# Sharing batch 0's v casts among three engines, two tiles for batch 1's transposes, and a later place for batch 2's kv matmuls

## The chip, the cores and the metric

One core of one Trainium2 chip. The metric is the device time of one execution, in microseconds (us), median of several executions. Engines: PE (TensorE; PEld is its weight load), DVE (VectorE), ACT (ScalarE), POOL (GpSimd), SP (SyncE, which issues most transfers). The profiles below are of different executions, on several chips.

## The reference

Linear attention for 8 batches, 8 heads, 576 tokens, head size 64, then a feed-forward pair with exact Gelu:

```python
q_s = softmax(q, over head_dim);  k_s = softmax(k, over tokens)
kv  = einsum('bhsd,bhse->bhde', k_s, v)          # 64x64 for each head
x   = einsum('bhsd,bhde->bhse', q_s, kv)         # -> 4608 tokens x 512
out = gelu(x @ w_in) @ w_out                      # 512 -> 2048 -> 512, float32 in and out
```

## The kernel before

Everything is cast to bf16 on the chip. PE runs, for each batch of 512 tokens, 64 matmuls of the first layer (`h_phase`), 64 of the second (`y_phase`), and between them the small ones: 72 for kv, 8 for x, and for batches 0 and 1 also 16 transposes of q (the later batches get theirs by DMA). In the code, `ek` is exp(k), `qT` the transposed q, `xT` the transposed x, which the first layer reads. For batches 0 and 1 all of this must wait for first loads: q, k, v of batch 0, then the weights. The parts that the change touches, with cuts marked:

```python
def cast_v(b, hp, eng=nc.vector):              # v, f32 -> bf16, one pair of heads
    eng.tensor_copy(out=v_aug[b % 2][:, hp, :, 0:D],
                    in_=st[b]["vf"][:, hp, :].rearrange("p (n d) -> p n d", n=NS))

def tp_mm(b, half):                            # 8 transposes of q into PSUM
    ...
    if b == 1:
        if half == 0:
            st[b]["tp"] = psum_a.tile([128, 2, J, 2, 128], BF16, tag="a2", name="tp")
        ps = st[b]["tp"][:, half]              # both halves in one tile
    ...
# ---- the front
tp_mm(0, 0); tp_evac(0, 0, "s")
table(AF.Gelu)                                 # loads Gelu's table on ScalarE
warm(2)
cast_v(0, 0)
for hp in range(1, HP):
    cast_v(0, hp, nc.gpsimd)
cast_wi(0, wi[0], "p"); cast_wi(1, wi[1], "p") # weight chunks 0, 1 on GpSimd
tp_mm(0, 1); warm(2)
...                                            # kv, x of batch 0, then the first layer
h_phase(0, {0: [cast_wi(2, "v")], 2: [cast_wi(3, "v")], ...})   # chunks 2 to 4 on VectorE
...
# ---- batch 1 in batch 0's second layer
tp_step(1, 0); tp_step(1, 1)                   # 8 transposes, copy out, twice
cast_v(1, 3)
y_part(12, range(J)); y_part(13, range(J))
kv_step(1)
...
y_phase(1, {(1, 12): [kv_step(2)], ...})       # batch 2's kv behind 29 matmuls
```

The softmax here doesn't subtract the row's maximum and nothing guards it: scores larger than these inputs give would overflow.

## Time and profile before

| | before |
|---|---|
| time, median of 6 runs | 281.69 us (281.43 to 282.00) |
| span of the profiled run | 280.1 us |
| PE busy | 271.0 us, 97% |
| first layer of batch 0 starts | 14.75 us |
| second layer of batch 0 starts | 29.29 us |
| batch 1's second eight transposes start | 41.05 us |
| batch 2's kv matmuls start | 66.92 us |

PE sets the time. What counts is when it starts each of its blocks, so the timeline of PE (start, duration, line, operation, count) is the view to read, and the other engines only where one of them releases PE. The lines at the three places are in the prediction below; three more:

```profile
29.29 10.52 PE L310 MATMUL ps<-wo_bf,g 128*128 128x512 bf16 x48
...
67.64 5.57 PE L310 MATMUL ps<-wo_bf,g 128*128 128x512 bf16 x25
73.14 0.63 PE L256 MATMUL ps<-qT,kvc 64*64 64x512 bf16 x8
```

A wide matmul (512 columns) occupies PE for 0.216 us from start to start; its listed 379 ns are its whole latency, pipelined.

### The profile page before, as it was taken

What the parts mean: (1) busy time and instruction counts of PE and PEld (TensorE: products, weight loads), DVE (VectorE), ACT (ScalarE), POOL (GpSimd) and SP (SyncE); (2) the same over time, 40 slices, a digit from 0 to 9 for tenths busy, and PEclk for the clock granted to TensorE, in tenths of its full rate; (3) what the DMA queues carried; (4) which work ended last, traced back from release to release, by engine and by line L of the source; (5) the groups of instructions that cost most, each with busy time, mean ns of one, the idle gap of its engine ahead of it and who ended that gap; (6) DMA issues with size and microseconds to landing.
All of it is one profiled execution on the core that took longest, in us unless ns stands there. A gap on an engine that the chain in (4) does not pass through costs nothing.

```text
span 280.1 us, 4564 instructions
## 1 busy us (share of the span) xinstructions
PE 271.0 (97%) x1922; PEld 125.2 (45%) x1922; DVE 102.2 (37%) x152; ACT 157.0 (56%) x243; POOL 33.0 (12%) x25
## 2 busy tenths in 40 slices
PE   7699989999999999999999999999999999999995
PEld 3344444444544444444444444444444444444443
DVE  3767477308763530074007500552005200230012
ACT  5747664779466915692469436852683264036400
POOL 1530050002020040005000500050005000000000
PEclk9999999999999999999999999999999999999999
DMA  6999999961997129911991189126501500120033
GB/s 235 380 404 427 400 401 407 399 250 43 268 390 91 41 76 240 357 41 42 259 372 41 42 209 375 53 77 171 131 0 75 150 2 0 75 77 0 0 77 76
DMA packets 44996, 50.10 MB, mean 179 GB/s; under 512 B 20400, under 2 KB 29872, under 8 KB 44720
## 3 DMA queue, kind: packets, MB, share of 16 engines
q1 hardware_dynamic: 44688, 49.68, 53.4%
q8 instruction: 15, 0.25, 0.4%
q10 hardware_dynamic: 288, 0.13, 0.2%
q14 instruction: 5, 0.04, 0.1%
HBM read 36.70 MB, written 9.44 MB: 165 GB/s over the span
## 4 chain that ended last, share of the span: by engine, by line
PE 75%; DMA 18%; SPq 2%; ACT 2%; ACTq 0%; issue 0%; DVE 0%
PE ps L310 36%; PE ps L300 35%; DMA w<-in_moe_w_in_dram 6%; DMA f<-in_v_dram 4%; DMA w<-in_moe_w_out_dram 3%; DMA out_dram<-y_sb 3%; SPq L98 2%; DMA touch<-in_moe_w_out_dram 2%; PE kv L166 1%; PE ps L332 1%; PE ps L256 1%; ACT ek L138 1%; ACT e L133 1%; ACTq L435 0%; ACT L133 0%
## 5 line engine op out<-in xcount | busy, mean ns | idle before, releaser
L300 PE MATMUL ps<-xT,wi_bf 128*128 128x512 bf16 x576 | 126.4, 379 | 0.2
L310 PE MATMUL ps<-wo_bf,g 128*128 128x512 bf16 x560 | 124.2, 379 | 0.0
L305 ACT ACTIVATE g<-ps 128x512 bf16<-128x512 f32 x144 | 85.2, 597 | 69.3 <-PE ps L300 69.3
L300 PEld LDWEIGHTS <-wi_bf 128*128 128x128 bf16 x576 | 56.1, 98 | 69.0 <-DVE wi_bf L383 1.0
L310 PEld LDWEIGHTS <-g 128*128 128x128 bf16 x560 | 54.0, 98 | 64.6 <-issue 0.8
L317 DVE COPY y_sb<-ps 128x512 f32<-128x512 f32 x35 | 23.8, 686 | 80.9 <-PE ps L310 80.7
L198 POOL TENSOR_TENSOR e<-e,recq 128x2048 bf16<-128x2048 bf16 (+1 forms) x9 | 25.7, 2857 | 179.2 <-DVE recq L197 151.0
L145 DVE CAST v_aug<-f 128x576 bf16<-128x576 f32 x26 | 17.9, 745 | 46.4 <-DMA f<-in_v_dram 46.4
L196 DVE TENSOR_REDUCE qsum<-e 128x16 f32<-128x1024 bf16 (+1 forms) x13 | 21.0, 1614 | 15.0 <-ACT e L133 15.0
L282 ACT CAST xT<-ps 128x512 bf16<-128x512 f32 x19 | 10.2, 589 | 27.9 <-PE ps L256 18.2
L133 ACT ACTIVATE e<-f 128x512 bf16<-128x512 f32 (+1 forms) x42 | 20.5, 556 | 2.4 <-DMA f<-in_q_dram 2.1
L138 ACT ACTIVATE ek<-f 128x2304 bf16<-128x2304 f32 (+1 forms) x10 | 17.2, 1730 | 1.9 <-DMA f<-in_k_dram 1.9
L280 DVE CAST xT<-ps 128x512 bf16<-128x512 f32 x15 | 9.7, 686 | 17.7 <-PE ps L256 14.8
L79 ACT ACT_TABLE_LOAD x9 | 11.5, 1283 | 2.8 <-issue 2.6
L133 ACT ACT_TABLE_LOAD x7 | 9.0, 1283 | 0.1
L417 PE MATMUL ps<-zeros 128*128 128x512 f32 (+1 forms) x14 | 7.1, 647 | 1.5 <-DVE zeros L449 1.5
L383 DVE CAST wi_bf<-w 128x512 bf16<-128x512 f32 x12 | 7.4, 660 | 2.5 <-DMA w<-in_moe_w_in_dram 2.2
L166 PEld LDWEIGHTS <-ek 64*64 64x64 bf16 x576 | 6.3, 105 | 3.0 <-issue 1.4
L166 PE MATMUL kv<-v_aug,ek 64*64 64x65 bf16 x576 | 6.9, 193 | 0.3
L198 DVE TENSOR_TENSOR e<-e,recq 128x1024 bf16<-128x1024 bf16 x4 | 6.4, 1608 | 0.1
L256 PE MATMUL ps<-qT,kvc 64*64 64x512 bf16 x60 | 5.0, 390 | 1.0 <-DVE kvc L177 1.0
L410 DVE CAST wo_bf<-w 128x2048 bf16<-128x2048 f32 (+1 forms) x4 | 4.4, 1090 | 3.8 <-DMA w<-in_moe_w_out_dram 3.8
(35 smaller groups left out, 42.4 us busy)
## 6 DMA issues: line engine op xcount, KB each, us to landing
out_dram<-y_sb SPq DMA_DIRECT2D x32, 256.0 KB, 2.3
f<-in_k_dram SPq DMA_DIRECT2D x6, 1152.0 KB, 9.7
f<-in_v_dram SPq DMA_DIRECT2D x6, 1152.0 KB, 11.8
f<-in_q_dram SPq DMA_DIRECT2D x6, 1024.0 KB, 7.5
w<-in_moe_w_in_dram SPq DMA_DIRECT2D x6, 512.0 KB, 8.9
f<-in_k_dram SPq DMA_DIRECT2D x4, 576.0 KB, 10.1
f<-in_v_dram SPq DMA_DIRECT2D x8, 288.0 KB, 7.9
f<-in_q_dram SPq DMA_DIRECT2D x4, 512.0 KB, 12.5
```

The costliest lines, as they stand in the source:

```text
L79: nc.scalar.activation(out=scr[:, 1:2], in_=scr[:, 0:1], func=func)
L133: nc.scalar.activation(out=dst[:, i], in_=src[:, u], func=AF.Exp)
L138: nc.scalar.activation(out=ek[b % 2][:, i:i + n], in_=st[b]["kf"][:, i:i + n].rearrange("p x (n d) -> p x n d", n=NS), func=AF.Exp,)
L145: eng.tensor_copy(out=v_aug[b % 2][:, hp, :, 0:D], in_=st[b]["vf"][:, hp, :].rearrange("p (n d) -> p n d", n=NS),)
L166: nc.tensor.matmul(ps[c, i, half, 0:D + 1], ek[b % 2][pr, hp, n, :], v_aug[b % 2][pr, hp, n, 0:D + 1], start=(n == 0), stop=(n == NS - 1),)
L196: nc.vector.reduce_sum(out=qsum, in_=eq[:, :, hs, :], axis=AX.X)
L198: eng.tensor_tensor(out=eq[:, :, hs, :], in0=eq[:, :, hs, :], in1=recq.unsqueeze(3).to_broadcast([128, J, w, D]), op=ALU.mult,)
L282: nc.scalar.copy(out=st[b]["xT"][:, hp, :], in_=ps)
L300: nc.tensor.matmul(ps, wi_bf[:, dm, t * 128:(t + 1) * 128], xT[:, dm, :], start=(dm == 0), stop=(dm == NDM - 1),)
L305: nc.scalar.activation(out=g[:, t, :], in_=ps, func=AF.Gelu)
L310: nc.tensor.matmul(ps, st[c]["g"][:, t, j * 128:(j + 1) * 128], wo_bf[:, t, :], start=(t == 0), stop=(t == NDF - 1),)
L317: nc.vector.tensor_copy(out=y_sb, in_=ps)
```

## The change

Three separate edits. (1) The front: batch 0's v casts go to POOL, DVE and ACT, so that each is cast as it lands; the last pair is loaded and cast in two token groups (5 and 4 of 9); Gelu's table load moves behind ACT's cast. (2) Batch 1's two halves of transposes get tiles of their own. (3) Batch 2's kv matmuls move two matmuls later.

```diff
-            nc.sync.dma_start(out=f[:, i * n:(i + 1) * n, :], in_=src[:, i * n:(i + 1) * n, :])
+            if b == 0 and name == "v" and i == parts - 1:
+                for c in (slice(0, 5 * D), slice(5 * D, NS * D)):
+                    nc.sync.dma_start(out=f[:, i, c], in_=src[:, i, c])
+            else:
+                nc.sync.dma_start(out=f[:, i * n:(i + 1) * n, :], in_=src[:, i * n:(i + 1) * n, :])
...
-    def cast_v(b, hp, eng=nc.vector):
+    def cast_v(b, hp, eng=nc.vector, n0=0, n1=NS):        # body: tokens n0 to n1, ACT by copy
...
-        if b == 1:
-            if half == 0:
-                st[b]["tp"] = psum_a.tile([128, 2, J, 2, 128], BF16, tag="a2", name="tp")
-            ps = st[b]["tp"][:, half]
+        if b == 1 and half == 1:
+            ps = psum_a.tile([128, 2, J, 2, 128], BF16, tag="a2", name="tp")[:, 0]
         else:                                              # half 0: psum_a, tag "a"
...
+    warm(2)
+    cast_v(0, 0, nc.gpsimd)
+    cast_v(0, 1)
+    cast_v(0, 2, nc.scalar)
+    cast_v(0, 3, nc.gpsimd, 0, 5)
+    cast_v(0, 3, nc.gpsimd, 5, NS)
     table(AF.Gelu)
-    warm(2)
-    cast_v(0, 0)
-    for hp in range(1, HP):
-        cast_v(0, hp, nc.gpsimd)
...
-        (1, 12): [lambda: kv_step(2)],
+        (1, 14): [lambda: kv_step(2)],
```

More of the change, by code (lines that the diff above doesn't have):

```diff
@@ L142, in exp_k @@
             )
-    def cast_v(b, hp, eng=nc.vector):
-        eng.tensor_copy(
-            out=v_aug[b % 2][:, hp, :, 0:D],
-            in_=st[b]["vf"][:, hp, :].rearrange("p (n d) -> p n d", n=NS),
-        )
+    def cast_v(b, hp, eng=nc.vector, n0=0, n1=NS):
+        o = v_aug[b % 2][:, hp, n0:n1, 0:D]
+        i = st[b]["vf"][:, hp, :].rearrange("p (n d) -> p n d", n=NS)[:, n0:n1]
+        if eng is nc.scalar:
+            eng.copy(out=o, in_=i)
+        else:
+            eng.tensor_copy(out=o, in_=i)
     def cast_v_all(b):
```

## The prediction

> **What bounds the kernel now.** I read the page first, then the timeline of TensorE (PE) alone, then the waits of three stretches.
>
> ```profile
> PE 271.0 (97%) x1922; PEld 125.2 (45%) x1922; DVE 102.2 (37%) x152; ACT 157.0 (56%) x243; POOL 33.0 (12%) x25
> PEclk9999999999999999999999999999999999999999
> ```
>
> PE is busy for 271 of 280 us at full clock. The change removes no large matmul, so it can only win idle time of PE, 280.1 - 271.0 = 9.1 us in all, half of it (4.6) in the first 15 us. From 77 us on, the timeline of PE shows blocks without a hole (64 matmuls of the first layer, 45 of the second, the small ones, 19 of the second, again and again). The change touches three places, all before 77 us, and a gain in any of them reaches the end only if no later wait before 77 us takes it back. So I treat each place as a gap and then look for the next wait behind it.
>
> Gap 1, the front, where v is cast and the first layer starts (timeline, columns: start us, duration us, engine, line, operation, operands, count, idle before it and its releaser):
>
> ```profile
> 11.13 2.16 POOL L145 CAST v_aug<-f 128x576 bf16<-128x576 f32 x3 [1.82 <-DMA f<-in_v_dram]
> 11.77 1.28 ACT L79 ACT_TABLE_LOAD   x1
> 13.34 0.36 PEld L166 LDWEIGHTS <-ek 64*64 64x64 bf16 x33 [0.28 <-issue]
> 13.37 1.07 ACT L282 CAST xT<-ps 128x512 bf16<-128x512 f32 x2
> 14.75 14.70 PE L300 MATMUL ps<-xT,wi_bf 128*128 128x512 bf16 x64
> ...
> 20.56 0.62 DVE L383 CAST wi_bf<-w 128x512 bf16<-128x512 f32 x1 [0.62 <-DMA w<-in_moe_w_in_dram]
> 21.81 1.16 DVE L383 CAST wi_bf<-w 128x512 bf16<-128x512 f32 x2
> 23.02 5.94 PEld L300 LDWEIGHTS <-wi_bf 128*128 128x128 bf16 x29 [0.42 <-DVE wi_bf L383]
> ```
>
> The second half of the kv matmuls waits for the third GpSimd cast, which ends at 13.29. But look at the last row: the 36th matmul of the first layer (29 are left) starts at 23.02, when the fourth VectorE cast of weight chunk 3 is done (21.81 + 1.16 = 22.97). That cast is the end of a row of casts that itself waited for the weight's transfer at 20.56. The DMA share in that stretch is full (table of stretches, 20 to 22 us: 1.06, 413 GB/s), and is near full from 3 us on. So **the moment 23.02 is set by the DMA stream**, not by the front.
>
> Gap 2, at the end of batch 0's second layer:
>
> ```profile
> 39.65 0.61 PE L217 MATMUL tp<-identity,e 128*128 128x128 bf16 x8
> 40.30 0.69 DVE L226 COPY qT<-tp 128x1024 bf16<-128x1024 bf16 x1 [0.66 <-PE tp L217]
> 41.05 0.61 PE L217 MATMUL tp<-identity,e 128*128 128x128 bf16 x8 [0.78 <-DVE qT L226]
> 41.49 1.89 PE L310 MATMUL ps<-wo_bf,g 128*128 128x512 bf16 x8
> 42.12 1.24 ACT L412 CAST wo_bf<-w 128x512 bf16<-128x512 f32 x2 [2.13 <-DMA w<-in_moe_w_out_dram]
> 42.30 0.74 DVE L145 CAST v_aug<-f 128x576 bf16<-128x576 f32 x1
> ```
>
> Batch 1's second half of transposes waits until VectorE has copied out the first half, since both halves lie in one tile.
>
> Gap 3, in batch 1's second layer:
>
> ```profile
> 60.38 6.42 PE L310 MATMUL ps<-wo_bf,g 128*128 128x512 bf16 x29
> 64.77 4.12 ACT L138 ACTIVATE ek<-f 128x2304 bf16<-128x2304 f32 x2
> 66.92 0.67 PEld L166 LDWEIGHTS <-ek 64*64 64x64 bf16 x72 [0.62 <-ACT ek L138]
> 66.92 0.78 PE L166 MATMUL kv<-v_aug,ek 64*64 64x65 bf16 x72
> ```
>
> Batch 2's kv matmuls arrive a little before ScalarE has finished the exponentials of k.
>
> **What the Trainium skill says.**
> - "ScalarE: Activation LUTs", section What ACT_TABLE_LOAD costs: about 1283 ns for a load plus about 1380 ns of drain at each switch. The trace agrees on the load (1.28 us), not on the drain: load at 11.77, next useful operation at 13.37, so 1.60 us with the 0.20 us dummy activation. I use 1.60.
> - "PSUM — Partial Sum Buffer", section PSUM bank collisions raise a hardware error: its rule is to guard by bank, as two engines in one bank and quadrant collide. One half of the transposes is 4 x 2 x 128 bf16 = 2 KiB, which that page gives as one bank. So the halves need not share a wait, and with tiles of their own the second half is free at once. The trace shows the wait (0.78 us).
> - "SBUF — State Buffer", section SBUF: two separate sides: VectorE and GpSimd share a port pair, and one of them can block for a whole instruction. In this trace the first weight cast on VectorE beside GpSimd's weight casts took 1.09 us where the others take 0.62. The new shared casts are spread by arrival, so I expect little of it.
> - "DMA: Bandwidth & Descriptors", Specifications: at least 512 B for line rate. The two new pieces of v have rows of 5 x 64 x 4 = 1280 B and 1024 B, so I expect no loss of rate.
>
> **The change part by part.**
>
> Front. The v parts land some 0.75 us apart: 295 KB at about 390 GB/s, and with the GpSimd start at 11.13 for part 1 this gives about 10.35, 11.1, 11.8 and 12.6. Today GpSimd casts parts 1 to 3 in 3 x 0.67 plus small gaps, hardly slower than they land. New: part 0 on GpSimd (10.4 to 11.1), part 1 on VectorE (11.15 to 11.9, 0.05 to 0.1 later than now), part 2 on ScalarE (about 0.65, from 11.85 to 12.5), part 3 in two pieces on GpSimd, ready near 13.0 instead of 13.29. The first half of kv moves about 0.1 later, and the second no longer waits for its cast. Now its last 34 matmuls run from 13.34; then it starts about 13.26 and all 36 take 0.47, done 13.73 instead of 13.82. That is a gain of **0.1 us before the xT copies**. Against it stands ScalarE: its table load moves from 11.77 to about 12.55, so the first xT copy goes from 13.37 to 12.55 + 1.60 = 14.15, and the copies end near 14.67, 15.21 and 15.8 (0.54 each for the pair, 0.59 for the last). The first layer needs the first xT (14.7, about its start now) and the weights of GpSimd (cast 13.96 to 14.6, set by DMA, unchanged); its third matmul waits for 15.27 instead of 15.18. So **the first layer begins 0 to 0.15 us later**. Does it matter? The 33rd matmul now starts at 21.87; without a wait the 36th would start 3 x 0.216 later, at 22.52, and it starts at 23.02. The slack is 0.50 us, and it swallows a delay of 0.15 as it would swallow any gain. The front is worth **0.0 us**. The extra DMA issue moves no bytes; a weight transfer takes 7 to 9 us from issue to landing at some 390 GB/s, so by my estimate about 3 MB are in flight and the queue does not run dry. I allow 0.0 to 0.15 us for a later landing of chunk 3.
>
> From 23.02 PE runs 29 + 48 matmuls without a gap (77 x 0.216 = 16.63, 23.02 + 16.63 = 39.65, as recorded), so the start of gap 2 stays at 39.65.
>
> Gap 2. Eight transposes occupy PE 41.49 - 41.05 = 0.44 us. The second eight could start at 39.65 + 0.44 = 40.09 instead of 41.05: **0.96 us won**, if nothing behind takes it back. Check: 8 second-layer matmuls (1.73) end at 42.26. Then come 72 kv matmuls, the first 36 of them (0.33) on parts already cast (GpSimd's last starts at 40.8). The others, from 42.6, need the last v cast: VectorE copies 40.30 to 40.99 and 40.99 to 41.68, then casts 41.7 to 42.45. This v part must have landed by 41.7. It was issued at 33.12 and the four parts take about 0.75 each; part 0 landed at 39.34, so the last lands at about 41.6. Just in time. The next second-layer matmuls (42.97) need ScalarE's weight cast that ends at 42.74, and the last ones (43.83) the one that ends at 43.36. Both hold with 0.2 to 0.5 us to spare. So I take 0.96.
>
> Gap 3. 29 x 0.216 = 6.26, 60.38 + 6.26 = 66.64, but kv starts at 66.92: 0.28 us idle. Moved two matmuls later, kv is due at 67.07 on this clock, after ek (64.77 + 2.06 = 66.83 and a hop). **0.28 us won**. ScalarE's chain hangs on PE's last first-layer matmul, so it moves with gap 2's gain. The kv result is wanted only at 73, so nothing is lost.
>
> Sum: 0.0 + 0.96 + 0.28 = 1.24 us. 281.68 - 1.24 = 280.44, rounded to 280.5 for the DMA allowance.
>
> **The rivals.**
> 1. The front costs more than its slack: the table load behind the cast is delayed further, because part 2 lands late or the port pair is contended, and the first layer starts over 0.5 us later. For: ScalarE has no spare time between 12.5 and 15.8. Against: 0.35 us of slack is left over by my sum. Time: 280.7 to 281.2.
> 2. Gap 2's gain turns into a wait for data. The last v part or the last weights of the second layer are DMA-bound (ScalarE waited 2.13 us for them), and if they land 0.3 to 0.8 us late, kv waits for the cast instead. Time: 280.7 to 281.3.
> 3. The front gains and the gain reaches the end, because the weight casts also come earlier. Against: VectorE waits for the transfer at 20.56. Time: 280.1.
> 4. The extra issue unsettles the weight stream, so chunk 3 lands later by up to a transfer of that part (0.75 us). Against: the DMA share is full and bytes are the same. Time: up to 281.2.
>
> **Range and chances.** Repeats of the kernel before spread over 0.25 us. Rivals 1, 2 and 4 reach up to 0.8 us above my number, rival 3 0.4 below it; so 280.0 to 281.2. A 2% change would be 5.6 us, far more than the three gaps together hold; within 2% has 0.98, the rest 0.01 each.
>
> **What would show it right or wrong.** Right: the second eight transposes of batch 1 start 0.44 us behind the first, with no wait on the VectorE copy; PE has no hole before batch 2's kv matmuls; the first layer of batch 0 still waits for VectorE's casts near 23.0, however its start moved; the table load sits near 12.5. Wrong: that wait has moved from 23.0 by more than 0.2, or PE waits for a v or weight cast between 40 and 45 us.

## The result, and the profile after

280.65 us median of 6 runs (280.41 to 281.56), against 281.69. Ratio of fast runs 0.9969, 95% interval 0.9952 to 0.9987. A ratio is always the mean time of one kernel's fast runs over that of the other's of the same rounds, so it is not quite the ratio of the medians. Here two of the six runs (281.32, 281.56) pull the mean up.

Timeline of PE, kernel after (line numbers have moved by 5 to 7):

```profile
14.82 14.65 PE L305 MATMUL ps<-xT,wi_bf 128*128 128x512 bf16 x64
29.32 10.52 PE L315 MATMUL ps<-wo_bf,g 128*128 128x512 bf16 x48
39.67 0.61 PE L222 MATMUL ps<-identity,e 128*128 128x128 bf16 x8
40.12 0.61 PE L222 MATMUL tp<-identity,e 128*128 128x128 bf16 x8
40.57 1.89 PE L315 MATMUL ps<-wo_bf,g 128*128 128x512 bf16 x8
...
59.45 6.85 PE L315 MATMUL ps<-wo_bf,g 128*128 128x512 bf16 x31
66.24 0.78 PE L173 MATMUL kv<-v_aug,ek 64*64 64x65 bf16 x72
66.95 5.14 PE L315 MATMUL ps<-wo_bf,g 128*128 128x512 bf16 x23
72.02 0.63 PE L261 MATMUL ps<-qT,kvc 64*64 64x512 bf16 x8
```

Subtract the rows from those of before. The second layer of batch 0 starts at 29.32 against 29.29: the front has given nothing. The eight second-layer matmuls behind the transposes start at 40.57 against 41.49: 0.92 earlier, or 0.95 measured from the start of the second layer (11.25 against 12.20). The second eight transposes now follow the first by 0.45 us and wait for nothing. From batch 1's second layer (59.45 against 60.38, still 0.93) to the block behind batch 2's kv (from 66.95; it was 67.64) another bit appears; at the x matmuls of batch 2 it is 72.02 against 73.14, so 1.12 in all. It stays so to the end: PE's last block starts at 271.96 against 273.07, 1.11 earlier.

The front itself, timeline of all engines, kernel after:

```profile
12.04 0.67 ACT L153 CAST v_aug<-f 128x576 bf16<-128x576 f32 x1
...
12.43 0.80 POOL L155 CAST v_aug<-f 128x320 bf16<-128x320 f32 x2 [1.22 <-DMA f<-in_v_dram]
...
12.72 1.28 ACT L79 ACT_TABLE_LOAD   x1
...
14.13 1.54 ACT L287 CAST xT<-ps 128x512 bf16<-128x512 f32 x3
...
20.59 4.95 DVE L388 CAST wi_bf<-w 128x512 bf16<-128x512 f32 x8 [0.57 <-DMA w<-in_moe_w_in_dram]
...
23.04 5.94 PEld L305 LDWEIGHTS <-wi_bf 128*128 128x128 bf16 x29 [0.43 <-DVE wi_bf L388]
```

The v casts are spread as intended and the table load has moved from 11.77 to 12.72. But the 36th matmul still waits for DVE's casts of weight chunk 3, until 23.04, and these still wait for the transfer (20.59).

### The profile page after: what moved, and what is told of

Same layout as the page of the kernel before. It is cut to its first block, busy times and chain, and to the rows that moved or that the text cites. A ratio compares the mean times of both kernels' runs of the same rounds, so it can differ in the third digit from the quotient of the medians.

```text
span 278.9 us, 4568 instructions
## 1 busy us (share of the span) xinstructions
PE 271.3 (97%) x1922; PEld 125.5 (45%) x1922; DVE 102.3 (37%) x152; ACT 157.4 (56%) x244; POOL 32.3 (12%) x25
## 4 chain that ended last, share of the span: by engine, by line
PE 91%; DMA 7%; DVE 1%; ACTq 0%; SPq 0%; issue 0%
PE ps L315 44%; PE ps L305 42%; DMA w<-in_moe_w_in_dram 3%; DMA f<-in_v_dram 2%; PE kv L173 2%; DMA touch<-in_moe_w_in_dram 2%; PE ps L261 1%; PE ps L337 1%; DVE wi_bf L388 0%; ACTq L440 0%; PE ps L266 0%; PE ps L222 0%; PE tp L222 0%; SPq L373 0%; DVE y_sb L342 0%
## 5 line engine op out<-in xcount | busy, mean ns | idle before, releaser
L79 ACT ACT_TABLE_LOAD x9 | 11.5, 1283 | 2.8 <-issue 2.6
L422 PE MATMUL ps<-zeros 128*128 128x512 f32 (+1 forms) x14 | 7.9, 703 | 1.4 <-DVE zeros L454 1.4
L138 ACT ACT_TABLE_LOAD x7 | 9.0, 1283 | 0.1
```

The lines of the kernel that those rows point to most:

```text
L79: nc.scalar.activation(out=scr[:, 1:2], in_=scr[:, 0:1], func=func)
L138: nc.scalar.activation(out=dst[:, i], in_=src[:, u], func=AF.Exp)
```

## The experiments

Twelve runs on three chips. The quickest way through them is one table of the profiled executions. Left out of it are the slow first try at gap 2, the large delay (its clock fell, see there) and the two runs that cut chunk 3 in halves. "Landing" is the start of POOL's first weight cast, which waits for weight chunk 0; "chunk 3" is the start of DVE's first cast of that chunk, which waits for its transfer; all in us.

| profile | landing | first layer starts | chunk 3 | second layer starts | first to second |
|---|---|---|---|---|---|
| before | 13.96 | 14.75 | 20.56 | 29.29 | 14.54 |
| after | 14.11 | 14.82 | 20.59 | 29.32 | 14.50 |
| kv move only | 14.09 | 14.87 | 19.86 | 28.89 | 14.02 |
| front only | 14.07 | 14.78 | 20.29 | 29.01 | 14.23 |
| all but front | 14.09 | 14.88 | 20.35 | 29.07 | 14.19 |
| no split transfer | 13.74 | 14.44 | 20.25 | 28.98 | 14.54 |
| small delay | 14.09 | 14.96 | 20.78 | 29.50 | 14.54 |
| large delay, PE kept busy | 13.95 | 16.32 | 20.38 | 30.39 | 14.07 |
| after, again | 13.94 | 14.65 | 19.84 | 28.67 | 14.02 |
| transposes only, again | 13.93 | 14.72 | 19.90 | 28.75 | 14.03 |

Every row obeys one rule, to 0.06 us: **the second layer starts at the later of (first layer's start + 14.02) and (chunk 3 + 8.73)**. Both constants come from the trace. 14.02 is 64 x 0.216 = 13.82 and one wait of 0.20 at the eighth column block (PE's weight load idles 0.32 us there, until 19.07 before and 19.14 after, just as the fourth Gelu ends and frees a bank: 18.42 + 0.60 and 18.49 + 0.60). 8.73 is four casts (2.41), a hop (0.05) and 29 matmuls (6.26). The executions differ in which of the two is later: 20.59 and 19.84 are two executions of the same kernel.

### Gap 2 alone, first try

```diff
 # the kernel before, with
-        if b == 1: ... ps = st[b]["tp"][:, half]
+        if b == 1 and half == 1:
+            ps = psum_a.tile([128, 2, J, 2, 128], BF16, tag="a2", name="tp")[:, 0]
```

> The kernel before with only gap 2 changed (batch 1's halves of transposes in two tiles). My theory: the second eight transposes start 0.44 us behind the first instead of 1.40, and the whole gain reaches the end: 0.93 to 0.96 us faster than before, ratio 0.9967. Rival (the gain turns into a wait for the v cast or the weights that come by DMA): 0.2 to 0.6 us faster, with a hole of PE between 42 and 45 us.

Inconclusive. Ratio 0.9986 (0.9955 to 1.0018), from runs of 280.68, 280.40, 281.49, 281.30 and 282.88 us. Its profiled run took 1010 us; nothing is read from it for the question (see the last section). It was run again, below.

### Gap 3 alone

```diff
 # the kernel before, with
-        (1, 12): [lambda: kv_step(2)],
+        (1, 14): [lambda: kv_step(2)],
```

> The kernel before with only the kv matmuls of batch 2 moved two matmuls later. As predicted: 0.28 us faster; as the profile after suggests, 0.19, because some 0.09 us of the gap is the change of instruction stream that PE has there without any wait. Rival (nothing, because a later wait takes it back): 0.0. All of it is near the noise of the times, so the start of the following second-layer matmuls relative to the start of the block decides: 7.26 us before, 7.07 (0.19 less) or 6.98 (0.28 less).

Ratio 0.9988 (0.9967 to 1.0009), median 281.43 beside 281.51 of before: not clear of noise by time. By the trace, from the start of batch 1's second layer to the x matmuls of batch 2 (which lie behind the same 54 wide and 72 small matmuls in both kernels): 59.97 to 72.53 = 12.56 us, against 60.38 to 73.14 = 12.76 before. So 0.20 is won, not 0.28. (The mark that the expectation names, the start of the second-layer matmuls behind kv, can't be read as it stands: two more wide matmuls lie before it now, and this trace lacks two records, 30 and 22 for 31 and 23.) The kernel with both edits (all but the front) shows the same 12.56, the front alone 12.76. Timeline of PE, kv move alone:

```profile
59.97 6.85 PE L310 MATMUL ps<-wo_bf,g 128*128 128x512 bf16 x30
66.75 0.78 PE L166 MATMUL kv<-v_aug,ek 64*64 64x65 bf16 x72
67.69 4.91 PE L310 MATMUL ps<-wo_bf,g 128*128 128x512 bf16 x22 [0.16 <-issue]
72.53 0.63 PE L256 MATMUL ps<-qT,kvc 64*64 64x512 bf16 x8
```

### The front alone

```diff
 # the changed kernel, with tp_mm as before and
-        (1, 14): [lambda: kv_step(2)],
+        (1, 12): [lambda: kv_step(2)],
```

> The kernel before with the front of the change alone (shared casts, split last pair, Gelu's table behind them). My theory: the first layer's 36th matmul still waits for VectorE's cast near 23.0 us, so 0.0 us, at most 0.1 slower. Rival (the front gains and it reaches the end): 0.2 us or more faster. Rival (the extra issue unsettles the transfers): some of the runs 0.7 to 1.0 us slower, as two of the six runs of the changed kernel were.

Ratio 1.0013 (0.9985 to 1.0040), median 281.82 beside 281.51 of before. Nothing won, as my theory says, and a gain of over 0.15% (0.4 us) is excluded. One of six runs was slow (283.30), but so was one of eleven of the kernel before on that chip (283.35): such stray runs need no extra issue.

### All but the front

```diff
 # the kernel before, with both edits above (gap 2 and gap 3)
```

> The changed kernel with its front undone (gap 2 and gap 3 alone). My theory: 1.12 to 1.24 us faster than before, the same as the changed kernel or 0.05 better. If the front is what makes some runs slow, this kernel has none of them and its mean is some 0.3 us below that of the changed kernel; if the front is worth something, it is slower than the changed kernel's fast group (280.4 to 280.7).

Median 280.62, ratio 0.9968 (0.9943 to 0.9994): the changed kernel's 0.9969 within the interval. Five runs lie at 280.35 to 280.67, one at 282.25. The whole gain is there without the front, and stray slow runs too.

### The last pair in one transfer

```diff
 # the changed kernel, with
-            if b == 0 and name == "v" and i == parts - 1:
+            if False:
```

> The changed kernel with v's last pair loaded in one transfer again (its two GpSimd casts kept). My theory: the second half of kv waits for the whole last part and its two casts, so it ends 0.1 to 0.3 us later; the first layer starts at most 0.2 later, and the second layer starts within the spread of 28.9 to 29.3 us that the weight transfers give anyway: same time as the changed kernel, 0.0. Rival (the extra issue is what makes some runs 0.7 to 1.0 us slower): no such run among these six and the mean 0.3 us lower.

Median 280.41 (280.19 to 280.80), ratio 0.9954 (0.9933 to 0.9975). No stray run here, which by itself would speak for the rival; but the small delay below keeps the split, on the same chip, and has none either (280.39 to 280.94), while all but the front, without the split, had one. The front's own mark, the first layer's start after the landing of weight chunk 0, is unharmed too: 14.44 - 13.74 = 0.70, against 0.71 with the split. The split buys nothing that this profile shows. Whether it costs anything in the mean stays open (0.9954 here, 0.9959 for the changed kernel on another chip; the intervals overlap nearly whole).

### A small delay in the front

```diff
     table(AF.Gelu)
+    nc.scalar.copy(out=junk[:, 0:256], in_=zeros[:, 0:256])
```

> The changed kernel with one more ScalarE copy of 256 columns (some 0.3 us) behind Gelu's table, so that the xT copies come 0.3 us later. My theory (slack of 0.46 us before the cast of weight chunk 3): the first layer starts 0.2 to 0.3 us later, the second layer not, the time is the same as the changed kernel's within 0.1 us. Rival (the front is on the path): 0.3 us slower, second layer starts at 29.6. If chunk 3 should land early in the profiled run (first cast of it by 20.0 us), the delay shows there even by my theory.

Median 280.57, ratio 0.9961 (0.9942 to 0.9980). ACT's xT copies start at 14.33 instead of 14.13, and the first layer 14.96 - 14.09 = 0.87 after the landing instead of 0.71. PE still waits for chunk 3's casts, and the second layer starts at chunk 3 + 8.72. So the delay of 0.16 was swallowed in this execution. That the second layer is at 29.50 and not 29.32 is the transfer (20.78 against 20.59), not the delay.

### A large delay in the front

```diff
     table(AF.Gelu)
+    3 x nc.scalar.copy(out=junk[:, 0:512], in_=zeros[:, 0:512])
```

> The changed kernel with three more ScalarE copies of 512 columns (some 1.6 us) at that place. My theory: the slack swallows 0.46 us and the rest reaches the end: the first layer starts 1.5 us later, PE no longer waits for VectorE's casts at 23 us, and the time is 1.0 to 1.2 us longer than the changed kernel's. Rival (no slack): 1.6 us longer. Rival (ScalarE's place in the front is idle time anyway): 0.3 us or less.

A miss for all three theories: 284.06 us, ratio 1.0084 (1.0059 to 1.0109), so 3.4 us more than the changed kernel's 280.65, for a delay of 1.67 (first layer's start after the landing: 16.73 - 14.35 = 2.38 instead of 0.71). The table of stretches (from:to, length, then busy time of PE, PEld, DVE, ACT and POOL with counts, granted clock, DMA share, GB/s) has the reason:

```profile
14.00:16.00 2.00, 0.52 (x12) 0.21 (x5) 1.16 (x3) 1.93 (x5) 1.51 (x3) 0.92 1.07 408
16.00:18.00 2.00, 1.27 (x4) 0.43 (x4) 1.63 (x3) 1.66 (x4) 0.93 (x2) 0.50 1.05 400
18.00:20.00 2.00, 2.00 (x6) 0.70 (x5) 0.99 (x2) 0.09 (x1) 0.00 (x0) 0.50 1.05 402
20.00:22.00 2.00, 2.00 (x6) 0.73 (x5) 1.76 (x4) 1.00 (x2) 0.00 (x0) 0.50 1.06 415
22.00:24.00 2.00, 1.96 (x9) 0.73 (x7) 1.78 (x5) 1.19 (x2) 0.00 (x0) 0.87 1.03 421
```

The granted clock fell to 0.50 in the hole that the delay opened (PE idle from 15.14 to 16.73), and stayed there for some 6.8 us (an estimate from the 0.92 and 0.87 of the stretches at its two ends). PE's weight loads then stand 0.43 us apart (17.11, 17.54, 17.97) instead of 0.216, for 14 matmuls: 14 x 0.21 = 3.0 us more. The second layer starts at 33.58, 2.83 behind 16.73 + 14.02. All six executions lost clock: three show a mean of 0.994 and took 283.3 to 283.7 us, three 0.986 to 0.988 and took 284.4 to 285.0, the profiled one among them. So the run did not measure the slack. The page "TensorE: Matmul & The Clock Gate", section What's actually happening, names this: a gate on PE's clock with half rate as its default, opened by activity. To keep the clock out, the next run fills the hole.

### The large delay with PE kept busy

```diff
 # the large delay, and
     x_mm(0, 1)
+    ps = psum_a.tile([128, 512], FP32, tag="a2", name="ps")
+    for i in range(7):
+        nc.tensor.matmul(ps, zeros[:, 0:128], zeros, start=True, stop=True)
```

> The large delay of ScalarE in the front again, with seven dummy matmuls of 512 columns (1.5 us) on PE in the gap that it opens, so that PE's granted clock stays at 1.0 (in the run before it fell to 0.5 from 16 to 22 us). My theory: the first layer starts 1.7 us later, the slack before weight chunk 3 swallows 0.46, so 1.2 us longer than the changed kernel: 281.9 us, with no wait on VectorE's casts of chunk 3. Rival (the delay costs more than itself for another reason than the clock): over 283 us again. Rival (no slack): 282.3 or more.

```profile
14.69 1.68 PE L497 MATMUL ps<-zeros 128*128 128x512 bf16 x7
16.32 14.23 PE L307 MATMUL ps<-xT,wi_bf 128*128 128x512 bf16 x64
30.39 10.52 PE L317 MATMUL ps<-wo_bf,g 128*128 128x512 bf16 x48
```

281.87 us, as expected, and the clock stays 1.00 throughout. The first layer starts 2.37 after the landing, 1.66 later than without the delay; the time is 281.88 - 280.53 = 1.35 us longer (means, against the changed kernel on the same chip). So 0.3 of the 1.66 was swallowed (0.2 by the medians, 281.87 - 280.38); I had expected 0.46. PE no longer waits for DVE's casts of chunk 3 (20.38 + 8.73 = 29.11 is past by then), and the second layer starts at 16.32 + 14.07. So the front is on the path once it is later than the transfer, and only then. The pair of runs also shows what the clock cost: 284.06 - 281.87 = 2.2 us of median (on two chips; the ratios to before, 1.0084 and 1.0007, give the same).

### The changed kernel again

```diff
 # no edit
```

> The changed kernel itself once more, on the chip of the others. My theory: 280.4 to 280.7, spread by where the transfers of the first 20 us land; runs of 281.3 and more, as two of six earlier, are chance and come for every kernel. Rival (the extra issue makes slow runs likelier): two or more of six runs above 281.2 again.

280.38 us median (280.16 to 281.38), ratio 0.9959 (0.9941 to 0.9977), one run of six above 281.2. In this execution chunk 3 landed 0.75 earlier than in the first, and two things change. Timeline of DVE, then of PE:

```profile
19.84 4.92 DVE L388 CAST wi_bf<-w 128x512 bf16<-128x512 f32 x8 [0.56 <-DMA w<-in_moe_w_in_dram]
...
41.36 0.75 DVE L155 CAST v_aug<-f 128x576 bf16<-128x576 f32 x1 [0.39 <-DMA f<-in_v_dram]
```

```profile
14.65 14.18 PE L305 MATMUL ps<-xT,wi_bf 128*128 128x512 bf16 x64
28.67 10.52 PE L315 MATMUL ps<-wo_bf,g 128*128 128x512 bf16 x48
...
41.74 0.90 PE L173 MATMUL kv<-v_aug,ek 64*64 64x65 bf16 x72
42.65 1.46 PE L315 MATMUL ps<-wo_bf,g 128*128 128x512 bf16 x6
```

The first layer is no longer set by the transfer (28.67 = 14.65 + 14.02), so here the front does set the second layer's start. And what PE is early by is given back in part at 41.7: batch 1's last v part lands at 41.36, kv waits for its cast, and from the transposes' matmuls to x it takes 39.92 to 44.04 = 4.12 us instead of 40.57 to 44.50 = 3.93. The transfers are the next bound again.

### Gap 2 alone, second try

```diff
 # as in the first try
```

> Gap 2 alone once more, since the first run's profile fell into a state of the chip in which every matmul took three times its time. From the profiles of the others (first-layer end to the next second-layer matmuls: 12.20 before, 11.25 with the change): 0.95 us faster than before, ratio 0.9966; the first run's 0.9986 was spoilt by one run of 282.9. Rival (gap 2 alone gives less than with the front beside it): ratio above 0.998 again.

Median 280.62 of five runs (280.44 to 280.70), ratio 0.9962 (0.9945 to 0.9978), 1.0 us. From the start of the second layer to the matmuls behind the transposes: 28.75 to 40.00 = 11.25, exactly that of the changed kernel:

```profile
28.75 10.52 PE L308 MATMUL ps<-wo_bf,g 128*128 128x512 bf16 x48
39.10 0.61 PE L215 MATMUL ps<-identity,e 128*128 128x128 bf16 x8
39.55 0.61 PE L215 MATMUL tp<-identity,e 128*128 128x128 bf16 x8
40.00 1.89 PE L308 MATMUL ps<-wo_bf,g 128*128 128x512 bf16 x8
```

The first try's 0.9986 came of three stray runs of five. Beside the changed kernel on the same chip (0.9959, median 280.38) all else in the change is worth 0.1 us by the ratios and 0.2 by the medians, not told from noise. The fronts compare directly: the first layer starts 14.72 - 13.93 = 0.79 after the landing here, and 0.71 with the new front, so the new front is 0.08 earlier.

### Weight chunk 3 in two halves

```diff
+        if i == 3:                       # load: columns 0:256 and 256:512 in turn
+            for u in (0, 256):
+                nc.sync.dma_start(out=w[:, :, u:u + 256], in_=src[:, :, u:u + 256])
 # cast_wi(3): two casts for each half of the columns; second layer's rows 1024 to 1535
 # loaded as pairs, as chunk 0's are, so that the order of the hidden units fits
```

> The changed kernel with weight chunk 3 loaded and cast in two halves of 256 columns (and the second layer's rows in the order that fits), so that the ninth and tenth column blocks need half the transfer and two casts instead of four. My theory (the wait near 23 us is for this chunk): the wait of 0.2 + 0.3 us goes, the second layer starts up to 0.5 us earlier (28.8 to 28.9), of which 0.3 to 0.5 reach the end: 280.2 us. Rival (transfers set it all the same, the wait only moves to the third or fourth half): 0.0.

280.60 us, ratio 0.9959 (0.9939 to 0.9979): no better. But the mechanism held. The second layer starts at 28.39, 14.02 after the first: no wait on chunk 3 is left, though it came late in this execution (20.91 + 8.73 would be 29.64). The gain then ran into the wait that my rival 2 named:

```profile
41.46 0.51 PE L173 MATMUL kv<-v_aug,ek 64*64 64x65 bf16 x38
42.40 0.47 PE L173 MATMUL kv<-v_aug,ek 64*64 64x65 bf16 x34 [0.43 <-DVE v_aug L155]
```

PE waits 0.43 us for the cast of batch 1's last v part, which landed at 41.59.

### Halves, and that v cast shared

```diff
 # the run before, without the split of batch 0's last pair, and
-    cast_v(1, 3)
+    cast_v(1, 3, nc.vector, 0, 5)
+    cast_v(1, 3, nc.scalar, 5, NS)
```

> An attempt at a better version: the changed kernel without the split transfer, with weight chunk 3 in halves, and batch 1's last v cast shared by VectorE (five token groups) and ScalarE (four), since in the run with the halves alone the half microsecond won near 23 us was lost at 42.4 us, waiting for that cast. My theory: the wait of 0.43 us shrinks to 0.1, so 0.2 to 0.4 us faster than with halves alone: 280.2 to 280.3. Rival (the transfers of the last v part and the last weights set that stretch whatever the casts do): 280.5, no better than the changed kernel.

280.51 us, ratio 0.9960 (0.9944 to 0.9976): no better than the changed kernel on the same chip (0.9959). The wait at kv is gone (72 matmuls in 0.78 us at 42.16), but in this execution weight chunk 0 landed later (14.32, first layer at 15.07), so PE was no earlier at that point. The rival holds so far as the times go; the profile doesn't tell whether the shared cast would have mattered in an early execution. No version tried here beats the changed kernel clear of noise.

## Why the prediction was right, point by point

1. **Gap 2: right in mechanism and size.** 0.96 predicted, 0.95 measured: 11.25 or 11.26 in all ten usable profiles with the edit, 12.20 in the three without it.
2. **"Just in time" for the last v part: right where the second layer starts at 29.3.** The cast ran from 41.53 to 42.27, kv from 42.39. In two profiles in which PE was earlier, rival 2 came true: 0.19 us lost in the changed kernel's second profile (second layer from 28.67), 0.43 with the halves (from 28.39). In the second try of gap 2 (from 28.75) the part had landed by 40.96 and nothing was lost: this landing varies too.
3. **Gap 3: mechanism right, the size off.** The mis-sized term is "60.38 + 6.26 = 66.64, but kv starts at 66.92: 0.28 us idle". All of it was taken for a wait. After the move, kv starts 66.24 - (59.45 + 31 x 0.216) = 0.10 us behind its due time with nothing to wait for. The kernel before has the same 0.09 ahead of batch 1's kv (41.49 + 8 x 0.216 = 43.22, start 43.31). So some 0.1 us is the changeover of PE between the two blocks, 0.2 was to be had, and 0.20 was measured.
4. **The front is worth 0.0: right, but its reason holds only in some executions.** The step "the moment 23.02 is set by the DMA stream, not by the front" is true of both first profiles and of the profiles of the front alone, all but the front, no split and small delay. In three others (kv move alone, after again, transposes again) chunk 3 landed by 19.9 and the front's own start set the second layer's. There its worth is the 0.08 us by which the new front starts earlier. It was luck that the two first profiles caught nearly the same landing (20.56 and 20.59): with the 19.84 of the second profile the second layer would have started 0.62 earlier (28.67 against 29.29), nearly all of it from the transfer, and it would have looked like the front's gain.
5. **Inside the front, two terms were wrong and hid each other.** The prediction had ACT's table load at 12.55 and the first xT copy 1.60 later, at 14.15; measured were 12.72 and 14.13. ACT's work before it ran later (k's second half landed at 9.83 instead of 9.69, the cast started at 12.04 instead of 11.85). And 1.60 was no cost of the table load: in the kernel before, the xT copy at 13.37 had been waiting for x matmuls that started at 12.92 and took 0.41. The load with its dummy activation costs 1.41. The predicted delay of the first layer by 0 to 0.15 did not come: it started 0.08 earlier after the landing than before. The gain of 0.1 us before the xT copies did come, seen from the landing: kv's second half ended at 13.87, 0.24 before it, and before the change at 13.82, 0.14 before it. And the new front can hardly go below its 0.71: PE's first weight load of the layer waits for GpSimd's cast of chunk 0 (0.23 us of idle time before 14.82, released by that cast), which waits for the landing.
6. **Rival 4 (the extra issue unsettles the weights)**: not shown. Chunk 3's landing varied from 19.84 to 20.59 in one kernel, and stray runs of 0.7 us and more came with and without the split. The five that lie furthest above their kernel's median, 1.4 us or more, outside the large delay (282.25, 282.88, 283.30, and 283.35 and 283.33 of the kernel before) have a mark of their own: a mean granted clock of 0.993 or 0.994, as three runs of the large delay have, where all other runs outside it, the one at 1010 us apart, show 0.997 or more. By an estimate, 0.006 x 280 = 1.7 us of PE's time. So these look like the clock and not like the transfers; none of them was profiled, and what made their clock fall stays open. The smaller strays, up to 1.0 us above, lack that mark.

The sum: 0.00 + 0.95 + 0.20 = 1.15, less 0.03 for the later transfer, is the 1.12 us of the trace; medians say 1.04 us at first and 1.21 the second time (281.59 - 280.38).

## What to carry to other kernels

Before a stage is made faster, write down the later of its own end and the landing of what comes next; where two such clocks lie within half a microsecond, look at several executions, since one profile shows only the clock that won that day. Where one engine waits to write the second half of a tile until another has copied out the first, try tiles of their own: here that was worth the whole wait, 0.95 us. And a delay experiment on PE must keep PE busy, or it may measure the clock, as here (284.06 against 281.87 us).

## What the Trainium skill lacked or had wrong

- "TensorE: Matmul & The Clock Gate" (sections What's actually happening and Why this matters for your kernels) speaks of an idle window of about 3.4 us before the half rate returns. Here the whole hole was 1.6 us long, and the clock fell some 0.5 us into it (mean clock 0.71 in the stretch from 15.6 to 15.8 us, 0.50 in the next; the hole began at 15.14). In the stretch from 12.2 to 15.6 us PE had been busy for 1.85 us, against 2.40 in the kernel after, which kept 1.00. So a half-busy stretch was enough; where the limit lies, these runs don't show. The page also tells of short idles between groups of matmuls that bring the half rate back, but gives no length for them.
- The same page (section Seeing it yourself) warns that the clock's records can be unreliable and that PE was seen at a quarter rate for over 50 us. One execution here stayed near that rate throughout, with a recorded clock of 1.0: 1008.6 us of span; 35 first-layer matmuls took 28.94 us, 0.83 each (3.8 times 0.216), while ACT's Gelu took its usual 597 ns. It was the first execution of the first try at gap 2; the other five took 280 to 283 us. Its cause is open. Page of that execution, groups of instructions:

```profile
L298 PE MATMUL ps<-xT,wi_bf 128*128 128x512 bf16 x566 | 470.0, 1109 | 5.2 <-issue 5.2
...
L303 ACT ACTIVATE g<-ps 128x512 bf16<-128x512 f32 x144 | 86.0, 597 | 502.4 <-PE ps L298 483.7
```

- "ScalarE: Activation LUTs", What ACT_TABLE_LOAD costs: 1283 ns agree with 1.28 us. The drain of 1380 ns was not there: from the load's start to the next copy it is 1.41 us, with a 0.20 us activation in it (12.72 to 14.13), and the cast before the load ended at 12.71.
- "DMA: Bandwidth & Descriptors" gives bandwidths and latencies, but we found nothing there on how much the landing of a transfer deep in a saturated queue varies between executions. Here a weight chunk some 6 MB into the stream (3.4 MB of q, k and v and 2.6 MB of weights by the kernel's sizes) was ready for its cast at 19.84 and at 20.59 us in two executions of one kernel, and that decided whether the transfer or the front set the start of the second layer.
